# Block-sorted attention with a bilinear FFN: batch 1's q and v turned on TensorE, loads issued in another order, the last output tile in two parts

## The chip, the cores and the metric

The kernel runs on one core of a Trainium2 chip. A core has TensorE (PE, matrix products into PSUM), VectorE (DVE), ScalarE (ACT), GpSimd (POOL) and SyncE (SP), each with its own instruction stream worked through in order, and 16 DMA engines shared by all of them. The metric is the device time in microseconds. Before the change the median of 8 runs is 255.94 us (255.31 to 256.87).

## The reference: what is computed

Four batches of eight heads, 768 positions, head size 64, eight blocks of 96 positions. A matrix `sort_net` (8 x 8 for each head) is normalised five times by rows and columns; it then mixes the blocks of k and v, block attention follows with the mixed blocks, and the result, as 3072 rows of 512, goes through a bilinear feed-forward network (FFN) of width 1536.

```python
for _ in range(5):
    P = exp(P - max(P, -1)); P = P / (sum(P, -1) + 1e-9); P = P / (sum(P, -2) + 1e-9)
k_sorted = einsum('bhij,bhjcd->bhicd', P, k_b);  v_sorted = einsum('bhij,bhjcd->bhicd', P, v_b)
scores = matmul(q_b, k_sorted_b.T) / 8
attn = softmax(scores)
x = matmul(attn, v_sorted_b)              # to 3072 x 512, heads beside one another
out = ((x @ w_a) * (x @ w_b)) @ w_out     # 512 -> 1536, 1536 -> 512
```

## The kernel before

Inputs are float32 in DRAM. GpSimd's loads cast them to bfloat16 on the way; the output is float32.

**Pairs of heads.** Attention works on two heads at a time. A pair has a number g from 0 to 15: batch g // 4, and pair g % 4 in it. The functions `stage_...` treat a whole pair of batches 1 to 3. Batch 0 is treated in two halves of four blocks each (`half_...`), so that the first FFN step can begin early. The steps of one pair:

- `stage_mix` (L265) multiplies the loaded k, and then the loaded v, by `s_all`, the spread-out mixing matrix: 12 matmuls each into a PSUM tile `mix` of pool psA. ACT copies k into `kT` in two halves; for v, DVE copies one half and ACT the other into `vT`. L283 then has SP start a DMA transpose of `vT` into `vs`.
- q must have its columns on partitions too. `pair_q` (L254) has POOL copy it into the order `qc`, and `stage_q` (L260) has SP start a DMA transpose into `qTf`. Batch 0 does both on TensorE instead (`half_q` L170, `half_v` L213): matmuls with the identity as moving operand write the transposes into PSUM tiles `q_ps` and `vs_ps`, which are copied out.
- `stage_scores` (L286): two halves of 8 matmuls into `sc` (psA), each followed by ACT's exponential into `eT`.
- `stage_o` (L301) with `one_o` (L236): two halves of 8 matmuls of `eT` with `vs` into `o_ps` (psA); DVE takes the reciprocal of the row sums (L245) and multiplies (L247) into `xp`.
- `to_xT` (L307): SP starts a DMA transpose of `xp` into the batch's `xT`.

**FFN.** `ffn_ab(b, m, t)` (L331) makes 128 of the 1536 columns for half t of batch b: four matmuls with w_a and four with w_b into two `pf` tiles of pool psF; ACT casts the first into `a_sb` (L343), DVE multiplies (L344) into `hT`. `ffn_out(b, c)` (L347) makes one output tile of 128 x 512: twelve matmuls into `po` (psF), a copy into `o_sb` by ACT (even c) or DVE (odd c, L162), and a store by SP. A batch has 24 `ffn_ab` and 6 `ffn_out`.

**PSUM.** Pool psA has 2 tiles of two banks (mix, scores, o), psF 4 tiles of one bank (`pf`, `po`, and the transposes of batch 0).

**Order.** The orders of PE, POOL and SP are written out by hand in the order of the calls; those of ACT and DVE are written out in the first part and placed by a scheduler later. While batch b's FFN runs, batch b+1's attention is done: `interleave` (L533) deals out the "units" of `units_full` (L505) among the FFN steps. The units of a batch are c (mixes of a pair, and its preparations for q and loads), s (scores) and o (with `to_xT`), in the order c s, c o s, c o s, c o s, o. Batch 1's units stand between the second half (t = 1) of batch 0's FFN; those of batches 2 and 3 between the whole FFN of batches 1 and 2. The FFN of batch 3 has no units.

**POOL's stream** carries all loads. After batch 0's q, k and v and the weights w_a and w_b come two pairs of batch 1, `spread` for heads 8 to 15 (it writes their part of `s_all`), w_out, two `pair_q`, the other two pairs of batch 1 and `spread` for heads 16 to 31. Every later pair is loaded from the unit c of the pair four before it. Tiles for k, v and q have 8 buffers each.

**Start.** Until `s_all` exists, PE has little to do. `keep_busy` (L164) issues matmuls of zeros whose result nobody reads: 8 first, then some in each round of the normalisation (L394), and `fill` of them ahead of some `half_mix` (L183, L188).

Of the kernel before, what the change touches and what calls it, by code (L numbers as in the profile page):

```python
# [9 lines left out]
FP32 = mybir.dt.float32  # L10
BF16 = mybir.dt.bfloat16
# [11 lines left out]
def kernel(  # L23
# [11 lines left out]
    nc = tc.nc  # L35
    P = 128
    B, H, S, D = q.shape
    NB = sort_net.shape[-1]
    BLK = S // NB
# [103 lines left out]
    def xT_of(b):  # L143
        if b not in xTs:
            xTs[b] = xtp.tile([P, KA, S], BF16, tag="xT", name="xT")
        return xTs[b]

    s_all = const.tile([P, BH, NB, CG], BF16, name="s_all")
    p_col = const.tile([P, NB, BH], BF16, name="p_col")

# [13 lines left out]
    def keep_busy(ps, n, cols=512):  # L164
        for _ in range(n):
            nc.tensor.matmul(ps[:, 0:cols], lhsT=warm[:, 0:P], rhs=warm[:, 0:cols],  # L166
                             start=True, stop=True)
# [84 lines left out]


    def pair_q(g):  # L254
        qc = qtp.tile([P, NCH, 2, D], BF16, tag="qc", name="qc", bufs=3)
        nc.gpsimd.tensor_copy(out=qc.rearrange("p c e d -> p e c d"),  # L256
                              in_=loaded[g][2].rearrange("p e (c d) -> p e c d", c=NCH))
        st[g, "qc"] = qc

    def stage_q(g):  # L260
        qT = qtp.tile([P, NCH, P], BF16, tag="qTf", name="qTf", bufs=3)
        nc.sync.dma_start_transpose(out=qT, in_=st[g, "qc"].rearrange("p c e d -> p (c e d)"))
        st[g, "qT"] = qT

    def stage_mix(g, what, engines):  # L265
        src2 = loaded[g][0 if what == "k" else 1]
        to = (kTs if what == "k" else vTs)[g % NBUF]
        pitch, whole = (BLK, S + PAD) if what == "k" else (P, NB * P)
        mix = psA.tile([P, 2, 512], FP32, tag="A", name="mix")
        for c in range(NCH):  # L270
            for e in range(2):
                nc.tensor.matmul(  # L272
                    mix[e * D:(e + 1) * D, c // 3, c % 3 * P:(c % 3 + 1) * P],
                    lhsT=src2[:, e, c * D:(c + 1) * D],
                    rhs=s_all[:, 2 * g + e], start=True, stop=True)
        for hf, eng in enumerate(engines):
            n = 2 // len(engines)
            for u in range(n):
                d1 = _ap(to, (hf + u) * 3 * CG, [[whole, P], [CG, 3], [pitch, NB], [1, CG]])
                s1 = _ap(mix, (hf + u) * 512, [[1024, P], [P, 3], [CG, NB], [1, CG]])  # L280
                copy(eng, d1, s1)
        if what == "v":
            nc.sync.dma_start_transpose(out=vss[g % NBUF][:, :, V0:V0 + P],  # L283
                                        in_=to.rearrange("p i t -> p (i t)"))

# [45 lines left out]
    def ffn_ab(b, m, t, begun=()):  # L331
        hT = hT_of(b)
        ab = []
        for n, w_sb in enumerate((w_a_sb, w_b_sb)):
# [6 lines left out]
            if n == 0:  # L341
# [2 lines left out]
        nc.vector.tensor_mul(out=hT[:, m, t * HW:(t + 1) * HW], in0=a_sb,  # L344
                             in1=ab[1][:, 0:HW])

    def ffn_out(b, c):  # L347
        hT = hTs[b]
        po = psF.tile([P, DMODEL], FP32, tag="F", name="po")
        for m in range(KO):  # L350
            nc.tensor.matmul(po, lhsT=hT[:, m, c * P:(c + 1) * P], rhs=w_out_sb[:, m, :],  # L351
                             start=(m == 0), stop=(m == KO - 1))
        o_sb = ffp.tile([P, DMODEL], FP32, tag="o_sb", name="o_sb", bufs=3)
        copy("act" if c % 2 == 0 else "dve", o_sb, po)
        if b == 0:
            h, u = divmod(c, 3)
            for c2 in range(2):
                nc.sync.dma_start(
                    out=_ap(out, (h * PH * NCH + 2 * u + c2) * DMODEL,
                            [[NCH * DMODEL, PH], [1, DMODEL]]),  # L360
                    in_=o_sb[c2 * PH:(c2 + 1) * PH])
        else:
            rows = out[b * S:(b + 1) * S, :].rearrange("(p c) n -> c p n", c=NCH)
            nc.sync.dma_start(out=rows[c], in_=o_sb)


    with tc.manual_schedule(engines={ET.PE, ET.Pool, ET.SP}):
        with tc.manual_schedule(engines={ET.Activation, ET.DVE}):
# [7 lines left out]
            for it in range(5):  # L376
                nc.scalar.activation(out=p_nat, in_=p_nat, func=AF.Exp)  # L377
                if it == 3:
                    half_q(0, 0, "act")
                    half_q(0, 1, "act")  # L380
                if it == 4:
                    half_q(0, 2, "act")
                    half_q(0, 3, "act")
                if it == 2:
                    with nc.allow_low_precision("sum of one one and zeros"):
                        nc.vector.reduce_sum(
                            out=mask, in_=_ap(ident, 0, [[P, P], [1, CG], [CG, NB]]),
                            axis=AX.X)
                nc.vector.reduce_sum(out=rsum, in_=p_nat, axis=AX.X)
                nc.vector.reciprocal(out=rsum, in_=rsum)  # L390
                if it > 0:
                    nc.tensor.matmul(heat[0:NB, 1, 0:NB], lhsT=rsum, rhs=rsum,
                                     start=True, stop=True)
                    keep_busy(heat[:, 0], (0, 4, 3, 2, 4)[it])  # L394
                nc.vector.tensor_mul(out=p_nat, in0=p_nat,
                                     in1=_ap(rsum, 0, [[NB, BH], [1, NB], [0, NB]]))
                nc.vector.reduce_sum(out=csum, in_=p_nat.transpose([0, 2, 1]), axis=AX.X)  # L397
                nc.vector.reciprocal(out=csum, in_=csum)
                if it < 4:
                    nc.vector.tensor_mul(out=p_nat, in0=p_nat,  # L400
                                         in1=_ap(csum, 0, [[NB, BH], [0, NB], [1, NB]]))
                else:
                    nc.vector.tensor_mul(
                        out=p_fin.bitcast(BF16).rearrange("h (i j u) -> h i j u", i=NB, j=NB),
                        in0=_ap(p_nat, 0, [[NB * NB, BH], [NB, NB], [1, NB], [0, 2]]),
                        in1=_ap(csum, 0, [[NB, BH], [0, NB], [1, NB], [0, 2]]))
# [20 lines left out]
            load_ab(2)  # L427
            load_ab(3)

            half_mix(0, 0, "k", "act", fill=2, cols=256)  # L430
            half_mix(0, 0, "v", "dve")
            to_columns(1)
            half_mix(0, 1, "k", "act")
# [2 lines left out]
            half_scores(0, 0)  # L436
            half_v(0, 0)
            half_mix(0, 1, "v", "dve")
            half_mix(0, 2, "k", "act", fill=1)
            half_o(0, 0)  # L440
            half_scores(0, 1)
            half_v(0, 1)
            half_mix(0, 2, "v", "act")
            half_mix(0, 3, "k", "act", fill=1)
            half_x(0, 0, "dve")
            half_o(0, 1)
            half_scores(0, 2)
            half_v(0, 2)
            half_mix(0, 3, "v", "act", fill=1)
            half_x(0, 1, "dve")  # L450
            half_o(0, 2)
            half_scores(0, 3)
# [12 lines left out]

        for c in range(4, 6):
            load_ab(c)
        for hp in range(2):
            load_pair(1, hp)
        spread(nc.gpsimd, p_col, 8, 8)  # L470
        for c in range(3):
            load_out(c)
        pair_q(HP)
        pair_q(HP + 1)
        for hp in range(2, HP):
            load_pair(1, hp)
        for g in range(2, 4):
            spread(nc.gpsimd, p_col, g * 8, 8)


        def units_half():
# [23 lines left out]
        def units_full(b):  # L505
            g0, us = b * HP, []

            def c_(g):
                if g == HP:
                    stage_q(g)  # L510
                if g + 1 < B * HP:
                    stage_q(g + 1)
                if g + 2 < B * HP:
                    pair_q(g + 2)
                if g + HP < B * HP:
                    load_pair((g + HP) // HP, g % HP)
                stage_mix(g, "k", ("act",))
                stage_mix(g, "v", ("dve", "act"))

            def o_(g):  # L520
                stage_o(g)
                to_xT(g)

            for n in range(HP + 1):
                if n < HP:
                    us.append(lambda g=g0 + n: c_(g))
                if n > 0:
                    us.append(lambda g=g0 + n - 1: o_(g))
                if n < HP:
                    us.append(lambda g=g0 + n: stage_scores(g))  # L530
            return us

        def interleave(steps, units, spare, slow=0):  # L533
            n, done = len(steps), 0
            for s, step in enumerate(steps):
                step()
                want = s + 1 if s < slow else -(-(s + 1) * len(units) // (n - spare))
                while done < min(want, len(units)):
                    units[done]()
                    done += 1  # L540

        steps = [lambda: ffn_ab(0, 0, 0, begun[0:2]), lambda: ffn_ab(0, 1, 0, begun[2:4]),
                 lambda: ffn_ab(0, 2, 0, begun[4:5])]
        steps += [lambda m=m: ffn_ab(0, m, 0) for m in range(3, KO)]
        interleave(steps, units_half(), 1, 3)

        steps = [lambda m=m: ffn_ab(0, m, 1) for m in range(KO)]
        steps += [lambda c=c: ffn_out(0, c) for c in range(NCH)]
        interleave(steps, units_full(1), 2)

        for b in range(1, B):
            steps = [lambda m=m, t=t, b=b: ffn_ab(b, m, t)
                     for m in range(KO) for t in range(2)]
            steps += [lambda c=c, b=b: ffn_out(b, c) for c in range(NCH)]
            interleave(steps, units_full(b + 1) if b + 1 < B else [], 2)


# [28 lines left out]
```

## Time and profile before

| what | value |
|---|---|
| median of 8 runs | 255.94 us (255.31 to 256.87) |
| the profiled execution: its time | 256.87 us |
| its span, first to last instruction | 255.1 us |
| PE busy | 239.7 us (94%) |
| PE weight loads | 136.1 us (53%) |
| DVE, ACT, POOL busy | 108.3, 102.4, 61.5 us |
| mean granted TensorE clock | 0.993 |
| bytes moved by DMA | 28.67 MB, of which POOL's loads 14.16 MB |

The profiled execution is the slowest of the eight; 1.8 us of its time lie outside the span. A busy share of PE counts a matmul from its start to its modelled end, and successive matmuls overlap, so prices of matmuls are best taken from one start to the next. The stages by time: start to 12 us (normalisation), first half of batch 0's attention to 24, its second half with the first half of its FFN to 47, batch 1's attention with the rest of batch 0's FFN to 95, batch 2's attention with batch 1's FFN to 150, batch 3's with batch 2's FFN to 204, batch 3's FFN and the last store to 255.

A view "by windows" gives, for each stretch, its length, and busy time and number of instructions of PE, PE's weight loads, DVE, ACT and POOL, then the granted clock, the DMA share and GB/s. A timeline line gives start, duration, engine, source line, operation, tile written and tiles read, shape and count, and in brackets the idle time before it and what ended it. A line of waits gives who waited for what: total us, times, longest us.

### The profile page before, as it was taken

How to read it: one execution, taken by the hardware profiler on the slowest of the kernel's cores; microseconds unless marked ns; L12 is line 12 of the kernel's file. 1: busy time of each engine (PE TensorE's matmuls, PEld its weight loads, DVE VectorE, ACT ScalarE, POOL GpSimd, SP SyncE). 2: the span in 40 equal slices, each digit the busy share in tenths (PEclk: the TensorE clock that was granted, in tenths of full speed). 3: DMA queues.
4: the chain of work that ended last, by engine and by line, in shares of the span. 5: the costliest groups of instructions: out<-in, count | busy, mean ns of one | idle time of the engine just before them, and what ended most of it. 6: DMA issues, size and time to landing. Idle time of an engine off the chain costs nothing.

```text
span 255.1 us, 5503 instructions
## 1 busy us (share of the span) xinstructions
PE 239.7 (94%) x2250; PEld 136.1 (53%) x2250; DVE 108.3 (42%) x259; ACT 102.4 (40%) x202; POOL 61.5 (24%) x83
## 2 busy tenths in 40 slices
PE   7889899989986699999999999999999999999993
PEld 2466566556542246666664456666654455665441
DVE  6764456535531214455462224545443144444111
ACT  3365555566613006554732036374541033333010
POOL 8965678562825102601100000000000000000000
PEclk9999999999999799999999999999999999999999
DMA  6999999999999997994322444233213310000132
GB/s 82 200 200 197 197 202 200 173 191 148 186 139 152 193 239 148 142 116 84 62 56 60 141 126 78 44 70 66 41 35 108 131 41 0 0 3 1 43 121 82
DMA packets 56441, 28.67 MB, mean 112 GB/s; under 512 B 33376, under 2 KB 53344, under 8 KB 56416
## 3 DMA queue, kind: packets, MB, share of 16 engines
q0 software_dynamic: 20944, 14.16, 41.4%
q1 hardware_dynamic: 35472, 14.17, 28.5%
q8 instruction: 17, 0.28, 0.4%
q14 instruction: 8, 0.07, 0.1%
HBM read 28.32 MB, written 6.29 MB: 136 GB/s over the span
## 4 chain that ended last, share of the span: by engine, by line
PE 82%; DMA 9%; DVE 5%; ACT 1%; issue 1%; DVEq 0%
PE pf L323 46%; PE po L351 23%; DMA vs<-vT 9%; PE mix L272 3%; PE o_ps L241 3%; PE sc L293 2%; PE mixh L191 2%; PE sc L206 1%; PE vs_ps L218 1%; PE xt_ps L232 1%; DMA p_nat<-in_sort_net_dram 1%; DVE hT L344 1%; DVE xph L247 1%; DVE csum L397 1%; ACT p_nat L377 1%
## 5 line engine op out<-in xcount | busy, mean ns | idle before, releaser
L344 DVE TENSOR_TENSOR hT<-a_sb,pf 128x384 bf16<-128x384 bf16 x95 | 52.6, 553 | 73.8 <-PE pf L323 46.1
L323 PE MATMUL pf<-xT,w_a_sb 128*128 128x384 bf16 x380 | 77.9, 327 | 0.0
L323 PE MATMUL pf<-xT,w_b_sb 128*128 128x384 bf16 x380 | 77.5, 326 | 0.0
L343 ACT CAST a_sb<-pf 128x384 bf16<-128x384 f32 x95 | 45.5, 479 | 65.1 <-PE pf L323 48.6
L351 PE MATMUL po<-w_out_sb,hT 128*128 128x512 bf16 x288 | 65.3, 386 | 0.0
L323 PEld LDWEIGHTS <-w_b_sb 128*128 128x128 bf16 x384 | 37.5, 98 | 24.9 <-issue 0.3
L323 PEld LDWEIGHTS <-w_a_sb 128*128 128x128 bf16 x384 | 34.6, 98 | 22.1
L351 PEld LDWEIGHTS <-hT 128*128 128x128 bf16 x288 | 28.0, 99 | 33.6 <-issue 2.2
L162 DVE COPY o_sb<-po 128x512 f32<-128x512 f32 x12 | 8.3, 691 | 48.4 <-PE po L351 31.6
L160 ACT COPY o_sb<-po 128x512 f32<-128x512 f32 x12 | 7.0, 585 | 49.5 <-PE po L351 44.9
L256 POOL COPY qc<-q 128x768 bf16<-128x768 bf16 x12 | 9.9, 825 | 55.2 <-DMA qTf<-qc 37.4
L298 ACT ACTIVATE eT<-sc 96x768 bf16<-96x768 f32 x24 | 18.0, 802 | 8.6 <-PE sc L293 8.6
L241 PE MATMUL o_ps<-vs,eT 96*128 96x65 bf16 x256 | 11.2, 193 | 7.6 <-DMA vs<-vT 7.0
L241 PEld LDWEIGHTS <-eT 96*128 96x128 bf16 x256 | 10.0, 97 | 10.9 <-issue 8.0
L247 DVE TENSOR_TENSOR xp<-o_ps,rec 96x512 bf16<-96x512 f32 x24 | 15.5, 678 | 0.1
L160 ACT CAST kT<-mix 128x384 bf16<-128x384 f32 x24 | 10.3, 482 | 6.0 <-PE mix L272 6.0
L94 POOL DMA_DIRECT2D v<-in_v_dram x16 | 11.6, 727 | 1.5 <-DMA w_a_sb<-in_moe_w_a_dram 0.6
L94 POOL DMA_DIRECT2D k<-in_k_dram x16 | 11.6, 724 | 1.4 <-DMA w_a_sb<-in_moe_w_a_dram 0.8
L245 DVE RECIPROCAL rec<-o_ps 96x8 f32<-96x8 f32 x32 | 5.3, 187 | 13.4 <-PE o_ps L241 13.3
L166 PE MATMUL heat<-warm 128*128 128x512 bf16 x21 | 8.0, 526 | 1.3 <-DVE warm L77 1.3
L94 POOL DMA_DIRECT2D q<-in_q_dram x12 | 8.7, 729 | 1.3 <-DMA w_a_sb<-in_moe_w_a_dram 0.6
L210 ACT ACTIVATE eT<-sc 96x768 bf16<-96x768 f32 x8 | 6.5, 808 | 3.2 <-PE sc L206 3.2
(71 smaller groups left out, 139.5 us busy)
## 6 DMA issues: line engine op xcount, KB each, us to landing
out_dram<-o_sb SPq DMA_DIRECT2D x18, 256.0 KB, 2.0
k<-in_k_dram POOLq DMA_DIRECT2D x16, 192.0 KB, 8.0
v<-in_v_dram POOLq DMA_DIRECT2D x16, 192.0 KB, 8.5
q<-in_q_dram POOLq DMA_DIRECT2D x12, 192.0 KB, 9.7
w_a_sb<-in_moe_w_a_dram POOLq DMA_DIRECT2D x6, 256.0 KB, 10.6
w_b_sb<-in_moe_w_b_dram POOLq DMA_DIRECT2D x6, 256.0 KB, 10.7
w_out_sb<-in_moe_w_out_dram POOLq DMA_DIRECT2D x3, 512.0 KB, 10.8
out_dram<-o_sb SPq DMA_DIRECT2D x12, 128.0 KB, 6.5
```

The costliest lines, as they stand in the source:

```text
L94: nc.gpsimd.dma_start(out=to, in_=_ap(t, base, [[W, P], [S * D, 2], [1, W]]))
L160: nc.scalar.copy(out=out, in_=in_)
L162: nc.vector.tensor_copy(out=out, in_=in_)
L166: nc.tensor.matmul(ps[:, 0:cols], lhsT=warm[:, 0:P], rhs=warm[:, 0:cols], start=True, stop=True)
L241: nc.tensor.matmul(o_ps[:, e, i * (D + 1):(i + 1) * (D + 1)], lhsT=eT[:, hf, e, i * BLK:i * BLK + P], rhs=vs[0:BLK, i0 + i, V0 - 1 + e * ( ...
L247: nc.vector.tensor_tensor(out=_ap(xp, i0 * 2 * D, [[nxp * 2 * D, BLK], [D, 2], [2 * D, NBH], [1, D]]), in0=_ap(o_ps, 1, [[1024, BLK], [511 ...
L256: nc.gpsimd.tensor_copy(out=qc.rearrange("p c e d -> p e c d"), in_=loaded[g][2].rearrange("p e (c d) -> p e c d", c=NCH))
L298: nc.scalar.activation(out=eT[:, hf, :, 0:HB], in_=sc[0:BLK, :, 0:HB], func=AF.Exp, scale=float(scale))
L323: nc.tensor.matmul(pf[:, 0:HW], lhsT=w_sb[:, kc, m * P:(m + 1) * P], rhs=x_cols(b, kc, t), start=(kc == 0), stop=(kc == KA - 1))
L343: nc.scalar.copy(out=a_sb, in_=pf[:, 0:HW])
L344: nc.vector.tensor_mul(out=hT[:, m, t * HW:(t + 1) * HW], in0=a_sb, in1=ab[1][:, 0:HW])
L351: nc.tensor.matmul(po, lhsT=hT[:, m, c * P:(c + 1) * P], rhs=w_out_sb[:, m, :], start=(m == 0), stop=(m == KO - 1))
```

## The change

Five things change.

1. For batch 1 (g from 4 to 7) q and v are transposed on TensorE, by the new `turn_q` and `turn_v`, with one DVE copy each; `pair_q`, `stage_q` and the transpose DMA of `vT` stay for batches 2 and 3.
2. Units are ordered c s, c s, o, c s, o, c s, o, o, and dealt out by `paced`, in which an output tile counts as two steps of `ffn_ab`.
3. POOL issues all loads of batch 1 ahead of w_out (with `spread` for batch 1 between them), then those of batch 2 at once, then `spread` for heads 16 to 23, four `pair_q` and `spread` for heads 24 to 31. A pair of batch 3 is loaded from unit c of the pair four before it, behind a POOL copy of one element of that pair's `kT` into `gate`. The DMA transposes of q are started from unit o: in batch 1's units those of batch 2, in later units those of batch 3.
4. The last output tile (batch 3, c = 5) is made in two parts: columns 0 to 383 copied by ACT and stored by SP, columns 384 to 511 copied by DVE and stored from ACT's queue.
5. Of the unused matmuls at the start, one more stands in each of the fourth and fifth rounds, the two ahead of the first mix have 512 columns instead of 256, and the three single ones further on are gone.

```diff
+    gate = const.tile([1, 1], BF16, name="gate")
...
-        qc = qtp.tile([P, NCH, 2, D], BF16, tag="qc", name="qc", bufs=3)
+        qc = qtp.tile([P, NCH, 2, D], BF16, tag="qc", name="qc", bufs=4)
...
-        qT = qtp.tile([P, NCH, P], BF16, tag="qTf", name="qTf", bufs=3)
+        qT = qtp.tile([P, NCH, P], BF16, tag="qTf", name="qTf", bufs=4)
...
+    def turn_q(g):
+        q2 = loaded[g][2]
+        q_ps = psF.tile([P, NCH, P], BF16, tag="F", name="q_ps")
+        for c in range(NCH):
+            for e in range(2):
+                nc.tensor.matmul(q_ps[e * D:(e + 1) * D, c, :],
+                                 lhsT=q2[:, e, c * D:(c + 1) * D],
+                                 rhs=ident, is_transpose=True)
+        qT = qtp.tile([P, NCH, P], BF16, tag="qT", name="qT")
+        nc.vector.tensor_copy(out=qT, in_=q_ps)
+        st[g, "qT"] = qT
+
+    def turn_v(g):
+        vT, vs = vTs[g % NBUF], vss[g % NBUF]
+        vs_ps = psF.tile([P, NB, P], BF16, tag="F", name="vs_ps")
+        for i in range(NB):
+            nc.tensor.matmul(vs_ps[:, i], lhsT=vT[:, i], rhs=ident, is_transpose=True)
+        nc.vector.tensor_copy(out=vs[0:BLK, :, V0:V0 + P], in_=vs_ps[0:BLK])
...
-        if what == "v":
+        if what == "v" and g >= 2 * HP:
             nc.sync.dma_start_transpose(out=vss[g % NBUF][:, :, V0:V0 + P],
...
+    def ffn_last(b, c):
+        hT = hTs[b]
+        rows = out[b * S:(b + 1) * S, :].rearrange("(p c) n -> c p n", c=NCH)
+        for n0, n1, eng, queue in ((0, 384, "act", nc.sync), (384, DMODEL, "dve", nc.scalar)):
+            po = psF.tile([P, 512], FP32, tag="F", name="po")
+            for m in range(KO):
+                nc.tensor.matmul(po[:, 0:n1 - n0], lhsT=hT[:, m, c * P:(c + 1) * P],
+                                 rhs=w_out_sb[:, m, n0:n1], start=(m == 0), stop=(m == KO - 1))
+            o_sb = ffp.tile([P, 512], FP32, tag="o_sb", name="o_sb", bufs=3)
+            copy(eng, o_sb[:, 0:n1 - n0], po[:, 0:n1 - n0])
+            queue.dma_start(out=rows[c][:, n0:n1], in_=o_sb[:, 0:n1 - n0])
+
     def ffn_out(b, c):
+        if b == B - 1 and c == NCH - 1:
+            ffn_last(b, c)
+            return
...
-                    keep_busy(heat[:, 0], (0, 4, 3, 2, 4)[it])
+                    keep_busy(heat[:, 0], (0, 4, 3, 3, 5)[it])
...
-            half_mix(0, 0, "k", "act", fill=2, cols=256)
+            half_mix(0, 0, "k", "act", fill=2)
...
-            half_mix(0, 2, "k", "act", fill=1)
+            half_mix(0, 2, "k", "act")
...
-            half_mix(0, 3, "k", "act", fill=1)
+            half_mix(0, 3, "k", "act")
...
-            half_mix(0, 3, "v", "act", fill=1)
+            half_mix(0, 3, "v", "act")
...
-        for hp in range(2):
+        for hp in range(3):
             load_pair(1, hp)
         spread(nc.gpsimd, p_col, 8, 8)
+        load_pair(1, 3)
         for c in range(3):
             load_out(c)
-        pair_q(HP)
-        pair_q(HP + 1)
-        for hp in range(2, HP):
-            load_pair(1, hp)
-        for g in range(2, 4):
-            spread(nc.gpsimd, p_col, g * 8, 8)
+        for hp in range(HP):
+            load_pair(2, hp)
+        spread(nc.gpsimd, p_col, 16, 8)
+        for g in range(2 * HP, 3 * HP):
+            pair_q(g)
+        spread(nc.gpsimd, p_col, 24, 8)
...
             def c_(g):
-                if g == HP:
-                    stage_q(g)
-                if g + 1 < B * HP:
-                    stage_q(g + 1)
-                if g + 2 < B * HP:
-                    pair_q(g + 2)
-                if g + HP < B * HP:
-                    load_pair((g + HP) // HP, g % HP)
+                if g < 2 * HP:
+                    turn_q(g)
                 stage_mix(g, "k", ("act",))
                 stage_mix(g, "v", ("dve", "act"))
+                if 2 * HP <= g < 3 * HP:
+                    nc.gpsimd.tensor_copy(out=gate, in_=kTs[g % NBUF][0:1, 0:1])
+                    load_pair(3, g % HP)
+
+            def s_(g):
+                stage_scores(g)
+                if g < 2 * HP:
+                    turn_v(g)
 
             def o_(g):
                 stage_o(g)
                 to_xT(g)
+                if g < 2 * HP:
+                    stage_q(g + HP)
+                if 3 * HP <= g + 3 < B * HP:
+                    pair_q(g + 3)
+                    stage_q(g + 3)
...
+        def paced(ab, po, units, spare):
+            steps = [(1, f) for f in ab] + [(2, f) for f in po]
+            total = sum(t for t, f in steps) - 2 * spare
+            now = done = 0
+            for t, step in steps:
+                step()
+                now += t
+                while done < len(units) and done * total < now * len(units):
+                    units[done]()
+                    done += 1
...
+        for b in range(B):
+            ab = [lambda m=m, t=t, b=b: ffn_ab(b, m, t)
+                  for m in range(KO) for t in range(2) if b > 0 or t == 1]
+            po = [lambda c=c, b=b: ffn_out(b, c) for c in range(NCH)]
+            paced(ab, po, units_full(b + 1) if b + 1 < B else [], 3 if b == 0 else 2)
```

More of the change, by code (lines that the diff above doesn't have):

```diff
@@ L526, in units_full @@
                     us.append(lambda g=g0 + n: c_(g))
+                    us.append(lambda g=g0 + n: s_(g))
                 if n > 0:
                     us.append(lambda g=g0 + n - 1: o_(g))
-                if n < HP:
-                    us.append(lambda g=g0 + n: stage_scores(g))
             return us
@@ L545 @@
         interleave(steps, units_half(), 1, 3)
[L547 to L555, printed above, removed]
+        for b in range(B):
[3 more added lines that the diff above has]
+            paced(ab, po, units_full(b + 1) if b + 1 < B else [], 3 if b == 0 else 2)
 _INS = ['q', 'k', 'v', 'sort_net', 'moe_w_a', 'moe_w_b', 'moe_w_out']
```

## The prediction

> **What bounds the kernel now.** I read the page's 40 slices first, then the waits, then busy time by stage, and last TensorE's timeline in the one stage that stood out.
>
> ```profile
> PE   7889899989986699999999999999999999999993
> PEclk9999999999999799999999999999999999999999
> DMA  6999999999999997994322444233213310000132
> PE o_ps L241 <- DMA vs<-vT: 7.0, 4, 4.5
> 46.80:95.10 48.30, 41.31 (x394) 22.26 (x392) 17.14 (x35) 18.19 (x36) 18.96 (x25) 0.96 1.39 174
> 95.10:149.80 54.70, 54.70 (x490) 31.52 (x489) 23.05 (x47) 23.89 (x47) 7.48 (x10) 1.00 0.59 105
> 149.80:204.30 54.50, 54.50 (x490) 31.36 (x488) 23.06 (x47) 23.89 (x47) 0.00 (x0) 1.00 0.32 75
> ```
>
> TensorE is full, except in slices 12 and 13, where its clock dips too. The wait view gives it one cause worth naming: o_ps waits for the DMA transpose of v. By stage: beside the FFN of batches 1 and 2 (95 to 204 us) PE is busy all the time; beside the second half of batch 0's FFN (46.8 to 95.1), where batch 1's attention runs, it isn't, with the DMA share at 1.39.
>
> ```profile
> 41.81 0.40 PE L218 MATMUL vs_ps<-ident,vT 128*128 128x128 bf16 x4
> 42.04 0.81 PE L323 MATMUL pf<-xT,w_a_sb 128*128 128x384 bf16 x4
> 48.20 0.53 PE L272 MATMUL mix<-s_all,k 128*64 128x128 bf16 x12
> 48.56 0.50 PE L272 MATMUL mix<-s_all,v 128*64 128x128 bf16 x12
> 49.00 0.82 PE L323 MATMUL pf<-xT,w_a_sb 128*128 128x384 bf16 x4
> 56.95 0.65 PE L241 MATMUL o_ps<-vs,eT 96*128 96x65 bf16 x16 [1.13 <-DMA vs<-vT]
> 64.58 0.65 PE L241 MATMUL o_ps<-vs,eT 96*128 96x65 bf16 x16 [0.28 <-DMA vs<-vT]
> 74.30 0.65 PE L241 MATMUL o_ps<-vs,eT 96*128 96x65 bf16 x16 [1.08 <-DMA vs<-vT]
> 85.19 0.73 PE L241 MATMUL o_ps<-vs,eT 96*128 96x65 bf16 x16 [4.50 <-DMA vs<-vT]
> ```
>
> Every pair of batch 1 stalls. I take prices from start to start, since records overlap: four 128-column transposes 0.23 us (57 ns each), twelve mix matmuls 0.36. The stage without stalls: 12 ffn_ab steps of 1.30 (eight pf at 162.5 ns), 6 output tiles of 2.59, four times mixes 0.90, scores 0.55 and o 0.49: 15.6 + 15.5 + 7.8 = 38.9. It took 48.3, so 9.4 are lost: 7.0 idle, 0.7 of matmul pipeline emptied four times, and some 1.7 of slow clock, because the 36 po matmuls after the longest stall took 9.4 instead of 7.8.
>
> **What the Trainium skill says.** "DMA: Bandwidth & Descriptors", section "Issuing engines are not separate DMA queues": transfers of all engines run on the same 16 DMA engines and interleave. The trace agrees: a v transpose lands in 3.0 us at best and 12.3 at worst, the worst beside POOL's loads. "TensorE: Matmul & The Clock Gate", section "HAM oscillation — how this bites in real kernels": a PE gap above about 3.4 us halves the clock. Agrees: only the 4.50 us gap is followed by slow matmuls. The same page, "Part 4: PE-mode transpose", gives some 275 ns for a transpose in a kernel; here the record is 219 ns but the next starts 57 ns later. I use the trace.
>
> **The change, part by part.**
>
> *Batch 1's transposes on TensorE.* Removed from the stage: qTf and vs transposes of pairs 4 to 7, thus all four stalls and the clock dip: -9.4. Added on PE per pair: turn_q, 12 transposes with 64-column weights in alternating halves, as the mixes: 0.36 plus a switch of about 0.04, so 0.40; not shown with this shape, between 0.30 (twelve 64-column q_ps at 27.20 to 27.51) and 0.78 (12 x 57 ns and a switch of 0.09). turn_v: 8 x 57 ns = 0.46 and a switch: 0.50, at most 0.55. Four pairs: +3.6 (3.1 to 5.3). DVE gets two copies per pair: 768 bf16 columns, about 0.55 us, and 96x1024, about 0.68 (from 384 columns 0.346 and 512 columns 0.42). That is 5 us on an engine busy 17 of 48: hidden.
>
> *Pacing.* The order becomes c, s, c, s, o, c, s, o, c, s, o, o, where s is now scores plus turn_v. In three pairs one or two ffn_ab steps (1.3 us each) stand between mix and scores, as one did before without a stall. Pair 7's c and s follow each other after the first output tile with nothing between. ACT then copies three halves, about 0.43 apart: kT done some 0.95 after mix k, its v half at 1.35. PE leaves mix v 0.4 after mix k, so scores' first half waits about 0.5 and its second, whose PSUM buffer is mix v's, about 0.2: +0.7 (0.4 to 1.2). Queued behind is only PE's own work. For small waits on the F buffers, which q_ps and vs_ps now share with pf and po, I add 0.3 (0 to 1). Stage: -9.4 + 3.6 + 0.7 + 0.3 = -4.8.
>
> *Loads.* On POOL batch 1's last pairs go ahead of w_out, batch 2 follows at once, spread for batch 1 goes one pair later (issued some 4 us later than 31.6, needed at 47), and pair_q of batch 2 and the other spreads come last. Before, q of pair 5 landed at 39.2; after it come 2 pairs of batch 1 (1.18 MB), w_out (1.57) and batch 2 (2.36): 5.1 MB at the 198 GB/s of that time, so loads end near 65 us instead of 97. Pair 7 is there by about 45 and mixed at 66; w_out by 53, used at about 66. SP gets qTf 8 to 11 in between batch 1's xT transposes; their q lands by 65, so they delay nothing by an estimate. xT of pair 7 must land before batch 1's FFN: o ends, two rec/xp of 0.84 on DVE, SP 1.25, landing 2.9 together under 6, against three output tiles of 7.8. Cover gone, each late microsecond counts in full. Batch 3's gated loads start with each mix of batch 2, as before: 0. The gate copy waits on ACT; behind it on POOL stand only that load and pair_q for batch 3.
>
> *Batches 1 and 2's FFN.* Same instructions, scores one unit earlier, o later. PE was full and stays so: 0. The last o comes one output tile later, leaving 7.8 us instead of 10.4 for the xT transpose.
>
> *Start.*
>
> ```profile
> 14.19 0.39 PE L166 MATMUL mixh<-warm 128*128 128x512 bf16 x1
> 16.09 0.39 PE L166 MATMUL mixh<-warm 128*128 128x512 bf16 x1
> 18.25 0.22 PE L206 MATMUL sc<-qT,kT 64*128 64x96 bf16 x2 [0.71 <-issue]
> 18.64 0.38 PE L166 MATMUL mixh<-warm 128*128 128x512 bf16 x1
> ```
>
> Three unused matmuls go, 0.31 each on PE with their switches: at most -0.93. Behind them ACT's exp and DVE's xph become the next limit: I follow mix, copy, scores, exp, o, xph for pairs 0 to 2 and find the o of pair 2 some 0.55 earlier. Two heat matmuls more lie in idle PE time (0.54 before 10.16, 0.23 before 11.55); the two wider fills end about when s_all does (12.15) and cost up to 0.1. Net -0.4 (-0.8 to +0.1).
>
> *Tail.*
>
> ```profile
> 248.51 0.58 ACT L160 COPY o_sb<-po 128x512 f32<-128x512 f32 x1 [4.59 <-PE po L351]
> 251.15 0.69 DVE L162 COPY o_sb<-po 128x512 f32<-128x512 f32 x1 [4.49 <-PE po L351]
> ```
>
> PE: 12 x (162.5 + 57) instead of 12 x 215.7 ns: +0.05, at most 0.3. The 384 columns go out on ACT and SP while PE does the rest. The last DVE copy has 128 columns: 512 took 0.69, 384 (the vT cast) 0.557, so 1.04 ns a column: 0.29, -0.40. The last transfer is 64 KB on ACT's queue, not 256 KB on SP's (2.0 us to landing; the 8 KB load of sort_net 1.6): 0 to -0.4, I take -0.15. ACT's queue isn't in this trace, and its first use may cost 0.5. Net -0.5 (-0.8 to +0.4).
>
> **Sum**: -4.8 - 0.4 - 0.5 = -5.7. The profiled execution has a span of 255.1 and took 256.87, the highest of the eight; it would come to a span of 249.4. I put the same difference to the median, 255.94: 250.2.
>
> **Rivals.**
> A, the above: 250.2, own range 249.0 to 251.4. Chance 0.66.
> B, TensorE pays more: turn_q unpaired, 5.3 in all, and waits of 1.2 at pair 7 plus 0.3 at each turn_v: 9.4 - 7.7 = 1.7 gained, and 0.3 at each end: 253.6. For it: psF has four buffers and each step of the stage will want up to four. Against: DVE and ACT are 35 to 38% busy in the stage. 0.20.
> C, the other side: SP is one queue, and qTf of pair 10 stands ahead of xT of pair 7. If batch 2's q still lands as late as loads end today (97 us; the DMA share is 1.01 there), qTf 10 leaves SP near 97 and xT 7 lands near 101; batch 1's FFN starts 6 later than today's 95.1, less 0.9 from both ends: 261. It decides once q of pair 10 lands after about 90. Against: loads end near 65 by bytes, with the competing transposes gone. 0.07.
> D, the removed matmuls kept the clock up: at half clock for one window of 3.4 us PE loses some 2 to 3: about 252.8. Against: the other PE gaps there are below 0.75. 0.04. No change at all, from a mix of B and D: 0.03.
>
> A measurement of this kernel can tell about 0.3% from no change. A, B and D are faster: 0.90; 0.03 same; C slower 0.07. The range takes A whole and B's better half: 248.9 to 252.9.
>
> **What would show it.** Stage from the first full-width mixes to batch 1's first pf: some 43.5 us, no wait of o_ps on vs there, clock 1.00; loads ended near 65; turn_q 0.40 and turn_v 0.50 start to start; one gap near 0.7 at pair 7's scores; last DVE copy near 0.29. I am wrong if PE waits for DVE copies at turn_v, if pf at batch 1's start waits for xT, or if the first 25 us are not shorter.

## The result, and the profile after

The changed kernel takes 252.49 us (median of 11 runs, 250.92 to 253.57); the kernel before, now with 32 runs, 256.24 (255.24 to 259.55). The ratio is 0.9856, with a 95% interval of 0.9832 to 0.9879: 3.7 us or 1.4% faster. 5.7 had been forecast.

First, from the page of the changed kernel, its span and the slices of PE, PE's clock and DMA (slices are counted from 0).

```profile
span 251.5 us, 5670 instructions
PE   7879999999998999999999999999999999999994
PEclk9995999999999999999999999999999999999999
DMA  6999999999623678565577733232124410000122
```

The hole of PE in slices 12 and 13 and the clock dip there are gone, and the DMA engines are no longer full from slice 10 (63 us) on. But a new dip stands in slice 3: from 19.0 to 25.8 us the clock is at half.

By stage, in the columns of the view by windows (length, busy PE, PE's weight loads, DVE, ACT, POOL, clock, DMA share, GB/s), for the first half of batch 0's attention, batch 1's attention, and the FFNs of batches 1 and 2:

```profile
12.20:26.90 14.70, 13.04 (x214) 9.01 (x213) 7.63 (x18) 6.66 (x12) 8.99 (x14) 0.77 1.42 198
49.30:92.40 43.10, 42.28 (x475) 25.34 (x473) 21.26 (x43) 18.31 (x36) 11.49 (x12) 1.00 0.76 127
92.40:147.10 54.70, 54.70 (x491) 31.50 (x490) 23.31 (x47) 23.79 (x47) 12.65 (x20) 1.00 0.66 123
147.10:201.60 54.50, 54.50 (x490) 31.40 (x489) 23.40 (x47) 23.79 (x47) 0.00 (x0) 1.00 0.29 68
```

The span shrank by 3.6 us, and it can be summed from the starts of the first matmul of each stage, before and after. Up to batch 1's stage: 46.81 to 49.35, +2.5. Batch 1's stage: 48.31 to 43.01, -5.3. The FFNs of batches 1 and 2: 109.20 to 109.21, nothing. From there to the end of the span: 50.78 to 49.93, -0.85. So the main part gave more than forecast, and the start took 2.5 back.

The start on PE's timeline after:

```profile
16.77 0.30 PE L207 MATMUL sc<-qT,kT 64*128 64x96 bf16 x6
18.52 0.22 PE L207 MATMUL sc<-qT,kT 64*128 64x96 bf16 x2 [1.44 <-issue]
19.76 0.64 PE L242 MATMUL o_ps<-vs,eT 96*128 96x65 bf16 x8
22.30 1.15 PE L343 MATMUL pf<-xT,w_a_sb 128*128 128x384 bf16 x3
```

The eight score matmuls of pair 2 are cut by a gap at the same matmul as before, but of 1.44 us instead of 0.71. After it everything is slow: three pf take 0.94 from start to start (23.24 follows 22.30). Before, they took 0.50:

```profile
21.46 0.66 PE L323 MATMUL pf<-xT,w_a_sb 128*128 128x384 bf16 x3
21.96 0.65 PE L323 MATMUL pf<-xT,w_b_sb 128*128 128x384 bf16 x3
```

The slow stretch isn't there in every run. The mean clock of each of the eleven runs orders their times: clock 1.000 gives 250.92; 0.991 to 0.993 give 251.79, 252.04, 252.31, 252.37 and 252.49; 0.986 gives 253.28 to 253.57 (five runs). A twelfth run on record, which the median leaves out, has clock 1.000 and 251.20. The profiled execution is one of those with 0.986.

### The profile page after: what moved, and what is told of

It reads as the page before. It is cut to its first block, busy times and chain, and to the rows that moved or that the text cites. A ratio compares the mean times of both kernels' runs of the same rounds, so it can differ in the third digit from the quotient of the medians.

```text
span 251.5 us, 5670 instructions
## 1 busy us (share of the span) xinstructions
PE 242.4 (96%) x2341; PEld 141.2 (56%) x2341; DVE 113.0 (45%) x267; ACT 102.8 (41%) x203; POOL 59.4 (24%) x83
## 4 chain that ended last, share of the span: by engine, by line
PE 92%; DVE 3%; ACT 2%; issue 1%; DMA 1%; DVEq 0%
PE pf L343 50%; PE po L386 24%; PE mix L292 4%; PE o_ps L242 3%; PE sc L313 2%; PE mixh L192 1%; PE heat L167 1%; PE po L373 1%; PE sc L207 1%; PE xt_ps L233 1%; PE vs_ps L282 1%; PE vs_ps L219 1%; PE q_ps L271 1%; DMA p_nat<-in_sort_net_dram 1%; DVE hT L364 1%
## 5 line engine op out<-in xcount | busy, mean ns | idle before, releaser
L343 PE MATMUL pf<-xT,w_a_sb 128*128 128x384 bf16 x380 | 78.9, 330 | 0.0
L386 PE MATMUL po<-w_out_sb,hT 128*128 128x512 bf16 x276 | 61.7, 379 | 0.0
L343 PEld LDWEIGHTS <-w_a_sb 128*128 128x128 bf16 x384 | 35.2, 98 | 22.6 <-issue 0.7
L386 PEld LDWEIGHTS <-hT 128*128 128x128 bf16 x276 | 26.4, 98 | 30.2
L161 ACT COPY o_sb<-po 128x512 f32<-128x512 f32 (+1 forms) x13 | 7.5, 577 | 50.5 <-PE po L386 49.1
L163 DVE COPY o_sb<-po 128x512 f32<-128x512 f32 (+1 forms) x12 | 7.9, 658 | 42.5 <-PE po L386 37.0
L550 POOL COPY gate<-kT 1x1 bf16<-1x1 bf16 x4 | 0.7, 178 | 51.4 <-ACT kT L161 51.4
L242 PEld LDWEIGHTS <-eT 96*128 96x128 bf16 x256 | 10.7, 100 | 3.6 <-ACT eT L211 1.0
L257 POOL COPY qc<-q 128x768 bf16<-128x768 bf16 x8 | 6.6, 844 | 6.5 <-DMA q<-in_q_dram 6.5
```

Of the source, the lines that this page charges most:

```text
L161: nc.scalar.copy(out=out, in_=in_)
L163: nc.vector.tensor_copy(out=out, in_=in_)
L242: nc.tensor.matmul(o_ps[:, e, i * (D + 1):(i + 1) * (D + 1)], lhsT=eT[:, hf, e, i * BLK:i * BLK + P], rhs=vs[0:BLK, i0 + i, V0 - 1 + e * ( ...
L343: nc.tensor.matmul(pf[:, 0:HW], lhsT=w_sb[:, kc, m * P:(m + 1) * P], rhs=x_cols(b, kc, t), start=(kc == 0), stop=(kc == KA - 1))
```

## The experiments

All ratios are to the kernel before on the same chip, with a 95% interval. Three chips were used, and the kernel before has another median on each: 254.95 us for experiments 1 to 4, 255.76 for 5, 6, 7 and 9, 256.02 for 8, 10 and 11. Medians of different experiments are therefore compared only beside what the traces show. In what follows a "fill" is an unused matmul ahead of a mix.

**1. The start undone, in the changed kernel.** All five edits of the start are taken back.

```diff
-                    keep_busy(heat[:, 0], (0, 4, 3, 3, 5)[it])
+                    keep_busy(heat[:, 0], (0, 4, 3, 2, 4)[it])
...
-            half_mix(0, 0, "k", "act", fill=2)
+            half_mix(0, 0, "k", "act", fill=2, cols=256)
...
-            half_mix(0, 2, "k", "act")
+            half_mix(0, 2, "k", "act", fill=1)
...
-            half_mix(0, 3, "k", "act")
+            half_mix(0, 3, "k", "act", fill=1)
...
-            half_mix(0, 3, "v", "act")
+            half_mix(0, 3, "v", "act", fill=1)
```

> The changed kernel with the whole start as before (heat counts, narrow fills, three single fills). Theory 1 (the removed fills let the TensorE clock fall in the first 25 us of most runs, and that ate the gain of the start): granted clock 1.00 or 0.99 in the first 27 us in every run, median 250.2 to 251.0, spread under 1 us, first full-width q_ps near 48.2 us. Theory 2 (the clock falls because the start phase varies from run to run, whatever the fills): spread of 2.5 us as in the changed kernel, median near 252.5.

Measured: 250.87 (250.70 to 251.27), ratio 0.9825 [0.9785, 0.9864], clock 0.999 or 1.000 in all six runs. Theory 1 holds: the runs lie within 0.6 us of one another, and the first full-width q_ps starts at 48.19. The rest of the change alone is worth 1.75%, which is still less than the 2.2% (5.7 of 255.94) forecast for the whole.

**2. The start alone, in the kernel before.** The reverse of the edit above.

> The kernel before with only the start's five edits. Theory 1: the start loses about 2.5 us when the clock falls and nothing when it does not; median 257 to 258.8, bimodal. Rival (prediction's own step): the start gains 0.4, median 255.8.

Measured: all six runs, 257.47 to 269.90 us (median 261.38, more than either expectation), are slower than all eleven of the kernel before (254.09 to 257.18). The ratio, 1.0123 [1.005, 1.020], takes the three fastest, with clocks of 0.972 to 0.987. So the start's edits by themselves make the kernel slower, by some 3 us in these three and by more in the others, and the gain of 0.4 doesn't show. How much of it is lost in the start isn't shown: the one profile is of a slower run (264.04 us) and has batch 1's stage 1.7 us late, at 48.50 instead of 46.81, but most of its loss in waits for v transposes there (7.88 and 2.32 us).

**3. Only the three single fills back.** The last three lines of edit 1 alone; more heat and wide fills stay.

> The changed kernel with only the three single fills back; more heat and wide fills stay. Theory 1: as the start wholly undone, 250.2 to 251.2, because it is the fills after S that hold the clock. Rival (the extra heat ahead of S shifts the clock window): stays near 252.5.

Measured: 251.15 (250.77 to 251.34), ratio 0.9832 [0.9792, 0.9872], clock 0.999 or 1.000 in all six. The time's interval overlaps the changed kernel's; what tells is the clock, which held in all six runs here. So it is the removal of these three that lets the clock fall; the extra heat ahead of `s_all` neither causes nor prevents it. Its profile has the gap too:

```profile
17.30 0.26 PE L207 MATMUL sc<-qT,kT 64*128 64x96 bf16 x4
18.77 0.26 PE L207 MATMUL sc<-qT,kT 64*128 64x96 bf16 x4 [1.21 <-issue]
```

A gap of 1.21 us didn't lower the clock, with fills ahead of and behind it.

**4. Eight more PE instructions at the very start.** In the changed kernel:

```diff
             keep_busy(heat[:, 0], 8)
+            keep_busy(heat[:, 0], 4, 8)
```

> The changed kernel with four unused matmuls of 8 columns more at the very start: eight more PE instructions ahead of everything. Theory F (the 1.44 us gap inside the scores of pair 2 is PE waiting for its next block of instructions, so it is tied to a place in the instruction stream): the gap moves four matmuls forward, between the second and third of the eight score matmuls, and ends again near 18.5 us. Rival (the gap belongs to that matmul, for instance a wait on kT or qT): it stays between the sixth and seventh.

```profile
17.19 0.22 PE L207 MATMUL sc<-qT,kT 64*128 64x96 bf16 x2
17.72 0.30 PE L207 MATMUL sc<-qT,kT 64*128 64x96 bf16 x6 [0.32 <-issue]
```

The gap moved forward by exactly four matmuls (each has a weight load, so eight instructions): from 6 + 2 to 2 + 6. It belongs to a place in the instruction stream and to no operand. Experiment 3 agrees: two fills, four instructions, stand ahead of it there, and it moved two matmuls, to 4 + 4. That it would end near 18.5 was wrong: it ended at 17.72 and was short, and the one run took 250.27 with a clock of 0.998.

What PE waits for there can be read from the traces, which record every DMA packet with its time, though no view prints single ones. On one queue of kind "instruction" packets of 16 KB arrive, 17 in the kernel before and 18 in the changed one, for 4500 and 4682 weight loads and matmuls of PE. In twelve of the thirteen profiles here the gap stands after PE's 446th or 447th of these instructions, and PE goes on 1.24 to 1.60 us after the first such packet has landed (all times in us):

| profile | PE arrives | packet landed | PE goes on |
|---|---|---|---|
| before | 17.54 | 16.79 | 18.25 |
| changed | 17.08 | 17.11 | 18.52 |
| experiment 3 | 17.56 | 17.39 | 18.77 |
| experiment 4 | 17.40 | 16.21 | 17.72 |
| experiment 6 | 17.79 | 17.06 | 18.49 |
| experiment 10 | 17.11 | 16.68 | 18.28 |
| experiment 11 | no gap | 14.20 | |

So, as far as these records show, PE waits in the gap for its next instructions: the gap ends when these have come, whenever PE arrives. The packet itself starts 3.4 to 4.1 us after PE has begun some 175th instruction, in all thirteen profiles (the 175th is the place that fits best). Instructions added ahead of everything let PE pass that place earlier, and the packet comes earlier.

**5. The last output tile alone, in the kernel before.** Only `ffn_last` and its call are added.

> The kernel before with only the last output tile in two parts. Theory (the changed kernel's trace: last DVE copy 0.29 instead of 0.69 us, last store 64 KB): 0.8 us faster, ratio 0.9965 to 0.9975. Rival (the prediction's sum, with a slower first use of ACT's queue): 0.5 faster or less, ratio 0.998 or above.

Measured: 254.47, ratio 0.9946 [0.9924, 0.9967]. It is faster, and the interval's upper end reaches into the first expectation. The kernel before varies by several microseconds through its DMA stalls, so the traces are the better ruler for the size. These are the last lines of the changed kernel:

```profile
247.75 0.48 ACT L161 COPY o_sb<-po 128x384 f32<-128x384 f32 x1 [1.41 <-PE po L373]
248.38 0.29 DVE L163 COPY o_sb<-po 128x128 f32<-128x128 f32 x1 [4.46 <-PE po L373]
248.70 0.38 ACTq L377 DMA_DIRECT2D out_dram<-o_sb  x1
```

The last copy takes 0.29 instead of 0.69 us, and from its end (248.67) to the end of the span pass 2.83 instead of 3.26 (255.1 less 251.84). The two gains make 0.83. Experiment 5's own profile ends alike: a copy of 0.29, and 2.8 us from its end.

**6. Three fills where PE waits anyway.** In the changed kernel, ahead of the last k mix of the first half, just before the gap:

```diff
-            half_mix(0, 3, "k", "act")
+            half_mix(0, 3, "k", "act", fill=3)
```

> The changed kernel with three unused matmuls of 512 columns ahead of the last k mix of the first half, just ahead of the place where PE waits for instructions. Theory (a long idle PE gap at 17 to 18.5 us lets the clock fall; fills that PE works off while it would wait anyway cost nothing): clock 1.00 in the first 27 us of every run, gap below 0.9 us, median about 1.5 us under the changed kernel, ratio to before 0.980 to 0.983. Rival (the fills after the gap are what holds the clock): clock still falls in some runs, ratio 0.986.

Measured: 250.98 (250.96 to 251.21), ratio 0.981 [0.9778, 0.9842], clock 0.998 to 1.000 in all six.

```profile
15.95 0.82 PE L167 MATMUL mixh<-warm 128*128 128x512 bf16 x3
17.53 0.26 PE L207 MATMUL sc<-qT,kT 64*128 64x96 bf16 x3
18.49 0.28 PE L207 MATMUL sc<-qT,kT 64*128 64x96 bf16 x5 [0.70 <-issue]
```

The fills cost PE 0.75 us (15.95 to 16.70), the gap became as much shorter (0.70 instead of 1.44), and its end stayed at 18.49. The rival, that the fills must stand behind the gap, falls. And the gap stood three matmuls forward, as six more instructions want it.

**7. Pair 7's mixes one step earlier.** The start as before; unit c of pair 7 is dealt out behind the last `ffn_ab`.

```diff
-            for t, step in steps:
+            for s, (t, step) in enumerate(steps):
                 step()
                 now += t
-                while done < len(units) and done * total < now * len(units):
+                want = now * len(units) / total
+                if spare == 3:
+                    want = (1, 2, 2, 3, 4, 4, 5, 6, 6, 7, 8, 9, 10, 11, 12)[min(s, 14)]
+                while done < len(units) and done < want:
```

> The changed kernel with the start as before and unit c of pair 7 dealt out one step earlier, after the last ffn_ab step, so that an output tile stands between its mixes and its scores. Theory (PE's 0.82 us at pair 7's scores is waiting for the copies of kT and vT): both waits gone, stage 42.2 instead of 43.1 us, 0.8 us under the same kernel without it. Rival (the wait comes back elsewhere, at o or at batch 1's first pf): no gain.

Measured: 250.01 (249.75 to 250.03), ratio 0.9765 [0.9736, 0.9794]. In the changed kernel and then in this one, pair 7's scores on PE's timeline:

```profile
77.14 0.34 PE L313 MATMUL sc<-qT,kT 64*128 64x96 bf16 x8 [0.62 <-DVE vT L163]
77.68 0.35 PE L313 MATMUL sc<-qT,kT 64*128 64x96 bf16 x8 [0.20 <-ACT vT L161]
```

```profile
71.28 2.76 PE L386 MATMUL po<-w_out_sb,hT 128*128 128x512 bf16 x12
73.98 0.51 PE L313 MATMUL sc<-qT,kT 64*128 64x96 bf16 x16
74.43 0.62 PE L282 MATMUL vs_ps<-ident,vT 128*128 128x128 bf16 x8
```

Both waits are gone, and batch 1's stage takes 42.05 us (46.78 to 88.83) instead of 43.01, which is the 0.62 + 0.20 that the trace showed and 0.14 more. The medians agree (250.87 in experiment 1, 250.01 here), though they are from two chips. No wait came back elsewhere.

**8. Batch 2's loads late, TensorE's transposes kept.** The start as before; each load of batch 2 goes back into unit c of the pair four before it, each `pair_q` into unit o.

```diff
-        for hp in range(HP):
-            load_pair(2, hp)
         spread(nc.gpsimd, p_col, 16, 8)
-        for g in range(2 * HP, 3 * HP):
-            pair_q(g)
...
                 if g < 2 * HP:
                     turn_q(g)
+                    load_pair(2, g % HP)
...
                 if g < 2 * HP:
+                    pair_q(g + HP)
                     stage_q(g + HP)
```

> The changed kernel with the start as before and batch 2's loads and q copies issued from the units of batch 1, as before, instead of all at once; q and v of batch 1 still turned on TensorE. Theory (only the transposes' place matters to PE): stage still 43 us, time within 0.3 us of the same kernel with early loads, ratio 0.981 to 0.984. Rival (early loads are needed so that xT of pair 7 lands in time): PE waits for xT at batch 1's first pf, 1 to 6 us lost, ratio 0.985 or more.

Measured: 250.99 (250.75 to 251.05), ratio 0.9801 [0.9765, 0.9837], against 0.9825 for the same kernel with early loads.

```profile
46.80:90.00 43.20, 42.38 (x475) 25.42 (x474) 21.26 (x43) 18.51 (x36) 10.22 (x14) 1.00 0.85 137
```

The stage is as full as in the changed kernel (42.4 of 43.2 us busy) and as long (47.06 to 90.06, 43.00 us), with the DMA share at 0.85. Once the transposes are on TensorE, the order of batch 2's loads is worth nothing that shows.

**9. Batch 2's loads early, the transposes left on DMA.** In the kernel before:

```diff
-        for hp in range(2):
+        for hp in range(3):
             load_pair(1, hp)
         spread(nc.gpsimd, p_col, 8, 8)
+        load_pair(1, 3)
         for c in range(3):
             load_out(c)
         pair_q(HP)
         pair_q(HP + 1)
-        for hp in range(2, HP):
-            load_pair(1, hp)
+        for hp in range(HP):
+            load_pair(2, hp)
...
-                if g + HP < B * HP:
+                if 3 * HP <= g + HP < B * HP:
```

> The kernel before with only batch 2's loads issued early, right behind w_out and two q copies; q and v of batch 1 still turned by DMA. Theory T (the transposes have to leave the DMA engines): pairs 4 and 5 stall as long as loads run, to about 65 us, so that 3 to 8 us are lost there; ratio 0.985 to 1.005. Rival L (the order of loads alone removes the stalls): stage near 39 to 41 us, ratio 0.965 to 0.975, better than the change.

Measured: 256.47, ratio 1.0051 [1.0032, 1.0071]: somewhat slower than before.

```profile
52.59 0.52 PE L293 MATMUL sc<-qTf,kT 64*128 64x96 bf16 x16 [2.40 <-DMA qTf<-qc]
53.04 1.42 PE L323 MATMUL pf<-xT,w_a_sb 128*128 128x384 bf16 x4
62.49 0.65 PE L241 MATMUL o_ps<-vs,eT 96*128 96x65 bf16 x16 [2.86 <-DMA vs<-vT]
```

Pair 4 now stalls twice while the loads run, at its scores for q's transpose and at its o for v's; pairs 5, 6 and 7 don't stall. The clock was at half for 3.41 us after each (four pf take 1.21 from start to start instead of 0.65), and the stage takes 47.85 us, near the 48.31 of before. Theory T had named pair 5 too; otherwise it holds. That the order of loads alone would do it is refuted.

**10 and 11. The best start.** The changed kernel with pair 7 apart (edit 7), without fills, and with 8 or 32 more PE instructions at the very start. The line for 32 (for 8 it ends in `4, 8`):

```diff
             keep_busy(heat[:, 0], 8)
+            keep_busy(heat[:, 0], 16, 8)
```

> The changed kernel with pair 7 apart and four unused matmuls of 8 columns (eight PE instructions) more at the very start. Theory F (the gap at the scores of pair 2 is a wait for instructions whose end depends on when PE passed an earlier place of the stream; eight instructions more let it pass that place earlier): gap 0.3 us ending near 17.7, clock 1.00, 0.4 us or more under the kernel with pair 7 apart and the fills: ratio 0.974 to 0.976. Rival (the short gap seen once was chance): gap 1.4 us in the profile, clock falls in some runs, ratio 0.977 to 0.982.

> The same with sixteen such matmuls (32 PE instructions). Theory F: the gap stands sixteen matmuls forward of where the changed kernel has it, within the mixes or o ahead of these scores, and is no longer than with eight; ratio 0.974 to 0.976. Rival: as the changed kernel with pair 7 apart, ratio 0.977 to 0.982.

Measured with 8: 250.11 (249.06 to 250.87), ratio 0.9767 [0.9727, 0.9807], clock below 0.995 in three of six runs. With 32: 248.83 (248.48 to 249.53), ratio 0.9724 [0.9689, 0.9758], clock 0.999 or 1.000 in all six. The scores of pair 2 with 8, and then with 32:

```profile
16.89 0.22 PE L207 MATMUL sc<-qT,kT 64*128 64x96 bf16 x2
18.28 0.30 PE L207 MATMUL sc<-qT,kT 64*128 64x96 bf16 x6 [1.17 <-issue]
```

```profile
17.20 0.41 PE L242 MATMUL o_ps<-vs,eT 96*128 96x65 bf16 x8
17.53 0.34 PE L207 MATMUL sc<-qT,kT 64*128 64x96 bf16 x8
17.81 0.40 PE L219 MATMUL vs_ps<-ident,vT 128*128 128x128 bf16 x4
```

With 8 the place is right, but the gap is long again, so a short gap can't be counted on. Theory F's cause still fits: in both profiles with 8, PE passes the 175th instruction at 11.8 us instead of 12.3 and the packet lands earlier than in the changed kernel, by 0.90 in experiment 4 and by 0.43 here. With 32 there is no gap, neither here nor at the place that theory F named for it, and the first pf stands at 20.95 instead of 22.30. There PE passes the 175th instruction at 9.7 us, still within the normalisation, and the packet lands at 14.20, well before PE needs it. This is the fastest version tried, by its median and by its span (247.5 us, against 248.0 in experiment 7); the two intervals overlap.

## Why the prediction was right, and where it failed

**Batch 1's stage: right in cause, by term nearly right in size.** It said -4.8 and 43.5 us; measured -5.3 and 43.0. In the changed kernel:

```profile
50.75 0.53 PE L271 MATMUL q_ps<-ident,q 128*64 128x128 bf16 x12
51.11 0.50 PE L292 MATMUL mix<-s_all,k 128*64 128x128 bf16 x12
53.73 0.62 PE L282 MATMUL vs_ps<-ident,vT 128*128 128x128 bf16 x8
54.19 0.81 PE L343 MATMUL pf<-xT,w_a_sb 128*128 128x384 bf16 x4
```

turn_q takes 0.36 from start to start (said: 0.40), turn_v 0.46 (0.50). Four pairs add at most 3.3 (3.6). The wait at pair 7 was said to be 0.5 + 0.2 and was 0.62 + 0.20. The 0.3 for the shared F buffers didn't occur: no PE wait in the stage names a DVE copy of qT or vs. DVE's two copies took 0.55 and 0.69 (said 0.55 and 0.68). All 9.4 us of stalls, emptied pipeline and slow clock went (5.3 + 3.3 + 0.8), as the first step of the sum had it. So rival B is out, and experiments 8 and 9 show that it was not the order of loads. The section "Part 4: PE-mode transpose" of the Trainium skill's page "TensorE: Matmul & The Clock Gate", with some 275 ns for one, would have put turn_v at an estimated 2.2 us (8 x 275) instead of 0.46.

One rival was not run: the new order of units with the transposes left on DMA, where o of the first three pairs comes later. By an estimate from starts it wouldn't have been enough with the loads of before. There pair 7's o began 16.5 us after its v mix (68.72 to 85.19), held up by the transpose; in the new order it begins after 8.1 (76.01 to 84.09). Together with experiment 9's loads it might have removed the stall of 2.86 us, but not the 2.40 at the scores of pair 4, which the new order moves no later.

**Loads: right.** The last q copy of batch 2 waited for its load until

```profile
64.56 0.83 POOL L257 COPY qc<-q 128x768 bf16<-128x768 bf16 x1 [2.15 <-DMA q<-in_q_dram]
```

and 65 had been said. xT of pair 7 landed in time: the three output tiles behind its o run on, and batch 1's first pf follows them directly (92.36). Rival C is out.

**The FFNs of batches 1 and 2: right,** 0.

**Tail: right in sign, too small.** It said -0.5 and was -0.85. The copy was exact. The term that was mis-sized is the last transfer: -0.15 was taken out of a range of 0 to -0.4; the time behind the last copy fell by 0.43. ACT's queue cost nothing that shows.

**Start: wrong.** It said -0.4 at best guess, with +0.1 as the worst, and was +2.5 in the profiled execution. Batch 1's stage began at 46.81 before and at 49.35 in the changed kernel; where the clock held and all or most of the start's edits stood, it began at 47.37, 47.03, 46.29 and 46.30 (experiments 3, 6, 4 and 11). The prediction had named this as a sign of being wrong, "if the first 25 us are not shorter". Two things failed in this step.

The smaller one: "the o of pair 2 some 0.55 earlier" was followed along mix, copy, scores, exp and o, with the gap of 0.71 us, which stood in the lines shown, carried along as a fixed length. It isn't fixed in length: PE arrived 0.46 earlier and was let on 0.27 later, because the packet with its next instructions landed later. So work taken out ahead of the gap is not gained, unless the packet comes earlier too. Where it did, in experiments 4 and 11, the stage began 0.5 earlier than before, near the -0.4 that had been forecast: the chain was right but for the gap.

The larger one: rival D, that the removed matmuls kept the clock up, got 0.04, with the argument that the other PE gaps there are below 0.75. But taking the fills out made that very gap twice as long. From 18.98 to 25.81 us the changed kernel's clock was at half, most of it in this line:

```profile
18.90:25.20 6.30, 6.25 (x61) 4.00 (x59) 2.98 (x7) 2.44 (x4) 3.27 (x5) 0.51 1.45 196
```

From the end of the gap to the start of batch 1's stage pass 28.56 us before, 28.60, 28.57 and 28.54 in experiments 3, 4 and 6, and 30.83 in the changed kernel. So the clock cost 2.3, and with the 0.27 of the gap that is the +2.5. D's own sum was off: one stretch of 3.4 us at half clock can cost at most 1.7. It cost 1.0 in experiment 10's profile (29.58 instead of 28.57); the changed kernel's profile has two stretches in a row.

The section "HAM oscillation — how this bites in real kernels" of the Trainium skill's page "TensorE: Matmul & The Clock Gate" speaks of PE gaps above some 3.4 us; here 1.44 us among short matmuls was followed by the fall in the profile, as were 2.40 and 2.86 in experiment 9's, and ten of eleven runs have a clock below 1. The measurement decides: a gap needn't be as long as that. What exactly the clock counts isn't shown; experiments 3 and 6 show that three 512-column matmuls near the gap are enough to hold it.

In sum: 5.7 were forecast. In the profile stage and tail gave 6.15, the later end of the gap took 0.3 and the clock 2.3, which leaves 3.6. That the median still lies within 248.9 to 252.9 is luck: the upper part of that range was meant for B, which didn't happen, and D, which did, was given 0.04.

## What to carry to other kernels

A transfer that PE waits for, on DMA engines that loads keep full, is best replaced by work on the engine that waits, if that is cheaper than the stall: 3.3 us of transposes bought 9.4 us of stalls, while another order of the loads only moved the stalls. An idle gap that the profile gives no releaser for ("issue") shouldn't be taken as a fixed length that moves with the work: count the instructions ahead of it in several versions, ask whether its end moves, and use the time for unused work rather than take work away ahead of it. Before unused matmuls are removed, add up what PE does in the microseconds around them, gaps included, and look at the clock of every run, not of the profiled one only.

## What the runs showed of the hardware that was not expected

- PE stopped for up to 1.44 us at one place of its instruction stream, after 446 or 447 weight loads and matmuls in twelve profiles, whatever work stood there; adding 4, 6 or 8 instructions ahead moved the stop by 2, 3 or 4 matmuls forward. It went on 1.24 to 1.60 us after a packet of 16 KB on an "instruction" queue had landed. Where that packet landed at 14.20 us instead of 16.2 to 17.4, there was no stop.
- The PE clock halved after idle times of 1.44, 1.17 (experiment 10), 2.40 and 2.86 us (experiment 9), each time for 3.41 us or twice that. It stayed at full speed after 1.21 us with fills around it (experiment 3), and in experiment 5's profile after 2.35 and 2.15 us with output tiles of 512 columns shortly ahead of them. So the length of the idle time alone doesn't decide; what does isn't shown.
- Twelve 128-column transposes with 64-column weights in alternating halves started 30 ns apart (0.36 us for twelve), eight with 128-column weights 57 ns apart.
